# Read-out tokens' first product as seven products, and the P runs of batches 0 and 1 regrouped

## The chip, the cores and the metric

The kernel runs on one core of a Trainium2 chip. The metric is the device time in microseconds of one execution; the median over several executions is given. The engines are TensorE (PE, matmuls; PEld, its weight loads), VectorE (DVE), ScalarE (ACT), GpSimd (POOL) and SyncE (SP, which here only issues DMAs). A matmul takes both operands from SBUF and writes to PSUM, which has eight banks of 128 x 512 float32; ACT and DVE read results out of PSUM.

## The reference

A cross-attention block between tokens `x` (8 batches, 8 heads, 512 tokens, 64 wide) and states `state` (8, 8, 32, 64), followed by a two-layer network with exact GELU over all 8 x (512 + 32) = 4352 rows of width 512:

```python
a = softmax(scale * x @ state.T);   xread = a @ state     # 512 rows per batch
a2 = softmax(scale * state @ x.T);  sread = a2 @ x        # 32 rows per batch
x2 = concat([xread, sread], axis=2)  # heads side by side: width 512
out = gelu(x2 @ w_in) @ w_out        # w_in 512 x 2048, w_out 2048 x 512
```

The 32 `sread` rows of each batch are called the read-out tokens: 256 over the whole problem.

## The kernel before, in words

**Tokens of x.** For a batch b the kernel never forms `xread`. It forms `P = state @ w_in` (`p_mm`, lines 415 to 428: 64-row, 32-column pieces of the array, one chunk `f` is 512 of the 2048 columns, two PSUM tiles per chunk) and copies it to SBUF in bf16 (`p_copy`: one half on ACT, one on DVE). `mm1` (line 460) multiplies a block of 128 columns of P with the transposed attention weights AT and applies GELU on ACT, giving `g`. `M(k, k+1)` is two such blocks. For batch 0 the second layer is the plain `mm2` or `mm2_m` (lines 486 and 515); `U(n)` is four matmuls of it. From batch 1 on the second layer is done with **seven products instead of eight** (Strassen's way, after Winograd: halves of the tokens, of the inner dimension and of the columns give 2 x 2 x 2 blocks; sums of blocks are multiplied). `X(b, name)` (line 599) is one of the seven, 16 matmuls of 128 x 256; `g_sum` (line 565) makes its left sum on DVE for every batch, `w_sums` (line 542) made the right sums once. Its evacuations add and subtract the products.

**Read-out tokens.** `sread` (line 378) computes them per batch, `sread_out` normalises, and `srt` (line 405) transposes them into `XSR`, which holds all 256 tokens as [128, 4 chunks of the model width, 32, 8]. After batch 7's are there, `mm1_sr(m)` (line 503) multiplies `w_in` with `XSR`: for each of 16 blocks of 128 columns, four matmuls of 128 x 256, then a GELU of 256 columns into `g_sr`. `R(name)` (line 734) does the second layer of the read-out tokens, again as seven products, from sums made by `r_sum`.

**Order.** Tiles are placed by pools that hand out buffers in a ring; the order of instructions on each engine is the order in which the program writes them, and each engine works through its own queue in order. PSUM has two families: `ftile` hands out four banks in turn (tag "f": `hp` of `mm1`, `p_ps`, `sr`, transposes, `st_ps`, `hps`), and `otile` the other four (accumulators of `mm2`, X and R). An instruction on PE that takes a bank waits until the last reader of what was there is done. Lines 809 to 943 write the order for batches 0 and 1 by hand; the loop of lines 945 to 1024 does batches 2 to 7 in eight slots p = 0 to 7 each, a slot being `M(k, k+1)` and one X product of the batch before. In batch 7 the slots p = 0 to 3 hold four calls of `mm1_sr` each, and p = 5 to 7 the R products.

**Early part that the change touches.** `p_run(1, (0, 1), ...)` makes chunks 0 and 1 of batch 1 (16 small matmuls, four "f" banks), `pmat(0, 3)` chunk 3 of batch 0, `pmat(1, 2)` chunk 2 of batch 1, with `mm2_m`, `atr(1)` (transposes of batch 1's attention weights), `M` and `srt(1)` between. `state_prep(2, 3)` transposes states into the "f" tile `st_ps` and copies them to `sbd` on DVE (line 165). `w_sums(0)` is a DVE sum that needs all of `w_out` (line 540), whose last quarter comes by the last DMA that `load_rest` issues. A block of P must be copied before the `mm1` that reads it: chunk 3 of batch 0 before M(12), chunk 0 of batch 1 before M(16), chunk 1 before M(20).

Of the kernel before, what the change touches and what calls it, by code (L numbers as in the profile page):

```python
# [9 lines left out]
FP32 = mybir.dt.float32  # L10
# [7 lines left out]
def kernel(  # L18
# [8 lines left out]
    nc = tc.nc  # L27
# [33 lines left out]
    def ftile(shape, name):  # L61
        return ps_f.tile(shape, FP32, name=name, tag="f")
# [297 lines left out]
    def atr(b, ts=(0, 1)):  # L360
        A = atts[b]
        if 0 in ts:
            A.AT = att.tile([128, SJ, 2, 128], BF16, name="AT", tag="AT")
        for t in ts:
            ps = ps_f.tile([128, SJ, 128], BF16, name="aT_ps", tag="f")
            for j in range(SJ):
                nc.tensor.transpose(ps[:, j, :], A.a[:, 2 * j + t, :], ident)
            nc.vector.tensor_copy(out=A.AT[:, :, t, :], in_=ps)
# [36 lines left out]
    def srt(b):  # L405
        A = atts[b]
        ps = ps_f.tile([128, HC, NS], BF16, name="srT", tag="f")
        nc.tensor.transpose(
            ps.rearrange("p c n -> p (c n)"), A.srm.rearrange("q t d -> q (t d)"), ident
        )  # L410
        nc.vector.tensor_copy(out=XSR[:, :, :, b], in_=ps)
# [23 lines left out]
    def pmat(b, f):  # L435
        p_copy(b, f, p_mm(b, f, ftile))

    def pmat00(h):
        if h == 0:
            Ps[0] = att.tile([128, 2, d_ff], BF16, name="P", tag="P")
        ps = [otile([128, 256], "p_ps") for t in range(2)]
        for c in range(HC):
            for t in range(2):
                nc.tensor.matmul(
                    ps[t][32 * c:32 * c + 32, :],
                    lhsT=sbd[64 * t:64 * t + 64, 0, c, 32 * t:32 * t + 32],
                    rhs=w_in_bf[64 * t:64 * t + 64, c, 256 * h:256 * h + 256],  # L450
                    start=True,
                    stop=True,
                )
        for t in range(2):
            nc.scalar.copy(out=Ps[0][:, t, 256 * h:256 * h + 256], in_=ps[t])
# [30 lines left out]
    def mm2(b, q, j):  # L486
# [11 lines left out]
        if q == 3:  # L498
            rows = out_rows(b, j)
            h = d_model // 2 if j == SJ - 1 else d_model  # L500
            evac(ps, [(rows[:, n:n + h], slice(0, 128), n, n + h) for n in range(0, d_model, h)])

    def mm1_sr(m):
        hp = ps_f.tile([128, B * NS], FP32, name="hps", tag="f")
        for c in range(HC):
            nc.tensor.matmul(  # L506
                hp,
                lhsT=w_in_bf[:, c, m * 128:(m + 1) * 128],
                rhs=XSR[:, c, :, :].rearrange("p n b -> p (n b)"),
                start=(c == 0),  # L510
                stop=(c == HC - 1),
            )
        nc.scalar.activation(out=g_sr[:, m, :], in_=hp, func=AF.Gelu)

    def mm2_m(b, m):
        for j in range(SJ):
            if m == 0:
                ops[b, j] = otile([128, d_model], "op")
            nc.tensor.matmul(  # L519
                ops[b, j],  # L520
                lhsT=gs[b][:, m, j * 128:(j + 1) * 128],
                rhs=w_out_bf[:, m, :],
                start=(m == 0),
                stop=(m == MC - 1),
            )
# [64 lines left out]
    def c22(b):  # L590
        xs[b, "v"] = c_tile("v")
        o = xs[b, "o", 1]
        nc.gpsimd.tensor_tensor(  # L593
            out=xs[b, "v"], in0=xs[b, "q"], in1=o[:, :, :NH], op=ALU.subtract
        )
        nc.vector.tensor_tensor(out=o[:, :, NH:], in0=xs[b, 3], in1=xs[b, "v"], op=ALU.add)  # L596
        x_out(b, 1)

# [103 lines left out]
    def L7():  # L702
        b = B - 1
        for j, n0, n1, at in PIECES:
# [4 lines left out]
            )  # L709
            rows_out(0, slice(j, j + 1), slice(n0, n1), nc.scalar if n0 else nc.sync)  # L710

    rs = {}

    def r_q(h, k):
# [86 lines left out]
    def M(*ms):  # L801
        for m in ms:
            mm1(m // MC, m % MC)

    def U(*us):
        for u in us:
            mm2(u // 16, u % 16 // 4, u % 4)

    begin(0)
    begin_e(0)  # L810
    keep_warm(31)
# [80 lines left out]
    sread_out(1)  # L892
    M(10, 11)
    mm2_m(0, 8)
    p_run(1, (0, 1), (None, None))
    mm2_m(0, 9)
    atr(1)
    pmat(0, 3)
    mm2_m(0, 10)
    M(16, 17)  # L900
    srt(1)
    M(12, 13)
    mm2_m(0, 11)
    begin(2)
    rearr(2)
# [4 lines left out]
    w_sums(0)  # L910
    M(14, 15)
    state_prep(2, 3)
    pmat(1, 2)
    U(12)
    begin(3)
    rearr(3)
# [28 lines left out]
    for b in range(2, B):  # L945
        nb = b + 1
        for p in range(8):
            k = 16 * b + 2 * p
            if p == 1 and nb < B:
                scores(nb, 0)  # L950
                scores(nb, 1)
            if p in (2, 3) and nb < B:
                norm(nb, p - 2)
            if p == 3 and nb + 1 < B:
                xtr_dma(nb + 1)
            if p == 5 and nb < B:
                atr_dma(nb)
            if p == 7 and nb < B:
                srt(b)
                if nb == B - 1:  # L960
                    srt(nb)
            M(k, k + 1)
            if b == 2 and p in (0, 3):
                pmat(2, 2 + p // 3)
            if b == 2 and p == 1:
                w_sums(4)
            if p < 5:
                if p == 0:
                    g_sum(b - 1, "5")
                X(b - 1, "45127"[p])  # L970
                if p < 3:
                    g_sum(b - 1, "127"[p])
            if nb == B and p < 4:
                for m in range(4 * p, 4 * p + 4):
                    mm1_sr(m)
            if p == 0 and b + 3 < B:
                hold_for(b, 0)
                load_x(4 if b == 2 else b + 3)
            if p == 6 and b == 2:
                hold_for(b, 12)  # L980
                load_x(5)
            if p == 0 and nb + 1 < B:
                begin(nb + 1)
                rearr(nb + 1)
            if nb == B:
                if p == 4:
                    r_homes()
                    r_sum("5")
                    r_sum("2")
                if p == 5:  # L990
                    g_sum(b, "6")
                    R("3")
                    r_sum("1")
                    R("4")
                    r_sum("6")
                    r_sum("7")
                if p == 6:
                    R("5")
                    X(b, "3")
                    R("2")  # L1000
                    R("1")
# [64 lines left out]
```

The softmax here doesn't subtract the row's maximum and nothing guards it: scores larger than these inputs give would overflow.

## Time and profile before

| | |
|---|---|
| median of 3 executions | 206.5 us (205.84 to 212.98) |
| the profiled execution | 206.31 us, of which 204.5 us from the first to the last instruction (the span) |
| PE, DVE, ACT, POOL busy | 97%, 70%, 66%, 34% of the span |
| `mm1_sr`'s 64 matmuls | first at 162.8, last at 177.5 us |
| granted TensorE clock | 1.00 throughout |

The page of a profile lists the busy time of each engine, then the span in 40 slices (a digit is the busy share in tenths), the DMA queues, the chain of work that ended last, the costliest groups of instructions and the DMA issues. A group's line gives the source line, the engine and operation, output and inputs by name, shapes, the number of instructions, their busy time and mean length, and what ended the idle time before them. Matmuls are pipelined: a matmul's own length contains its way through the array, so cost is read from the distance between starts, or from the chain, which counts each stretch once.

### The profile page before, as it was taken

What the parts mean: (1) busy time and instruction counts of PE and PEld (TensorE: products, weight loads), DVE (VectorE), ACT (ScalarE), POOL (GpSimd) and SP (SyncE); (2) the same over time, 40 slices, a digit from 0 to 9 for tenths busy, and PEclk for the clock granted to TensorE, in tenths of its full rate; (3) what the DMA queues carried; (4) which work ended last, traced back from release to release, by engine and by line L of the source; (5) the groups of instructions that cost most, each with busy time, mean ns of one, the idle gap of its engine ahead of it and who ended that gap; (6) DMA issues with size and microseconds to landing.
All of it is one profiled execution on the core that took longest, in us unless ns stands there. A gap on an engine that the chain in (4) does not pass through costs nothing.

```text
span 204.5 us, 4754 instructions
## 1 busy us (share of the span) xinstructions
PE 197.9 (97%) x1984; PEld 133.3 (65%) x1989; DVE 142.9 (70%) x227; ACT 134.0 (66%) x242; POOL 69.6 (34%) x76
## 2 busy tenths in 40 slices
PE   7799999999999999999999999999999999999993
PEld 2344444446777577766776687567775887778893
DVE  2953896689898959976797757765778543175882
ACT  3784685799686779666967596678857376744120
POOL 8983305334239546370527502420220011200000
PEclk9999999999999999999999999999999999999999
DMA  6999996995585788755783309470117001030125
GB/s 191 206 176 204 206 199 102 154 219 105 116 144 103 208 103 106 155 169 39 83 169 140 76 0 113 147 109 0 51 39 169 3 0 51 3 154 0 54 103 155
DMA packets 40565, 23.14 MB, mean 113 GB/s; under 512 B 21856, under 2 KB 39136, under 8 KB 40544
## 3 DMA queue, kind: packets, MB, share of 16 engines
q0 software_dynamic: 13984, 8.10, 29.7%
q1 hardware_dynamic: 25872, 14.36, 28.9%
q10 hardware_dynamic: 688, 0.39, 0.6%
q8 instruction: 15, 0.25, 0.5%
q14 instruction: 6, 0.05, 0.1%
HBM read 17.30 MB, written 8.91 MB: 128 GB/s over the span
## 4 chain that ended last, share of the span: by engine, by line
PE 88%; DMA 6%; DVE 2%; ACT 1%; POOL 0%; issue 0%; SPq 0%; DVEq 0%
PE xp L574 41%; PE hp L465 25%; PE p_ps L421 5%; DMA xb<-in_x_dram 4%; PE hps L506 3%; PE rp L750 3%; PE op L519 3%; DMA x0f<-in_x_dram 2%; PE op L491 2%; PE xp L680 2%; PE pt L330 2%; PE sr L384 1%; DVE a L353 1%; DVE cs L350 1%; PE xT_ps L256 1%; PE xT_ps L270 1%
## 5 line engine op out<-in xcount | busy, mean ns | idle before, releaser
L472 ACT ACTIVATE g<-hp 128x512 bf16<-128x512 f32 x124 | 67.3, 604 | 28.4 <-PE hp L465 21.6
L465 PE MATMUL hp<-AT,P 128*128 128x512 bf16 x248 | 63.6, 379 | 0.0
L574 PEld LDWEIGHTS <-gsum 128*128 128x128 bf16 x528 | 51.2, 98 | 13.1 <-issue 1.9
L568 DVE TENSOR_TENSOR gsum<-g 128x2048 bf16<-128x2048 bf16 x35 | 45.9, 1328 | 0.1
L574 PE MATMUL xp<-ws,gsum 128*128 128x256 bf16 x304 | 36.3, 273 | 0.0
L465 PEld LDWEIGHTS <-P 128*128 128x128 bf16 x248 | 22.9, 98 | 19.9 <-issue 2.8
L574 PE MATMUL xp<-ws,g 128*128 128x256 bf16 x224 | 26.8, 273 | 0.0
L574 PE MATMUL xp<-w_out_bf,gsum 128*128 128x256 bf16 x224 | 26.6, 273 | 0.0
L574 PEld LDWEIGHTS <-g 128*128 128x128 bf16 x224 | 21.8, 98 | 5.1 <-issue 0.2
L433 DVE CAST P<-p_ps 128x512 bf16<-128x512 f32 x30 | 19.6, 685 | 7.3 <-PE p_ps L421 7.2
L623 POOL TENSOR_TENSOR u<-s,oh 128x512 f32<-128x512 f32 x6 | 8.9, 1490 | 40.7 <-ACT oh L620 40.7
L224 POOL COPY x<-xb 128x1024 bf16<-128x1024 bf16 x12 | 13.1, 1118 | 21.0 <-DMA xb<-in_x_dram 21.0
L432 ACT CAST P<-p_ps 128x512 bf16<-128x512 f32 x30 | 16.8, 601 | 4.7 <-PE p_ps L421 4.3
L234 POOL COPY xo<-xb 128x1024 bf16<-128x1024 bf16 x12 | 14.7, 1251 | 4.4 <-PE sr L384 4.4
L593 POOL TENSOR_TENSOR v<-q,oh 128x512 f32<-128x512 f32 x6 | 8.8, 1460 | 20.8 <-ACT oh L625 17.6
L617 DVE TENSOR_TENSOR s<-xp,s 128x512 f32<-128x512 f32 x6 | 4.1, 691 | 11.3 <-PE xp L574 11.3
L519 PE MATMUL op<-w_out_bf,g 128*128 128x512 bf16 x45 | 11.4, 380 | 0.2
L421 PE MATMUL p_ps<-w_in_bf,sbd 64*32 64x512 bf16 x248 | 11.4, 383 | 0.1
L353 DVE TENSOR_TENSOR a<-e,ics 128x512 bf16<-128x512 bf16 x14 | 10.9, 782 | 0.5
L596 DVE TENSOR_TENSOR oh<-xp,v 128x512 f32<-128x512 f32 x6 | 4.1, 691 | 9.8 <-POOL v L593 9.8
L629 DVE TENSOR_TENSOR q<-xp,s 128x512 f32<-128x512 f32 x6 | 4.1, 684 | 8.0 <-PE xp L574 8.0
L350 DVE TENSOR_REDUCE cs<-e 128x16 f32<-128x512 bf16 x14 | 9.5, 676 | 0.0
(111 smaller groups left out, 217.4 us busy)
## 6 DMA issues: line engine op xcount, KB each, us to landing
out_dram<-oh SPq DMA_DIRECT2D x15, 256.0 KB, 2.4
xb<-in_x_dram POOLq DMA_DIRECT2D x7, 512.0 KB, 6.1
out_dram<-oh SPq DMA_DIRECT2D x6, 512.0 KB, 3.1
w_in_bf<-in_moe_w_in_dram POOLq DMA_DIRECT2D x6, 256.0 KB, 10.5
out_dram<-osb SPq DMA_DIRECT2D x5, 256.0 KB, 4.7
w_out_bf<-in_moe_w_out_dram POOLq DMA_DIRECT2D x4, 256.0 KB, 7.7
w_out_bf<-in_moe_w_out_dram POOLq DMA_DIRECT2D x2, 512.0 KB, 12.5
x0f<-in_x_dram SPq DMA_DIRECT2D x3, 256.0 KB, 3.9
```

Of the source, the lines that this page charges most:

```text
L224: nc.gpsimd.tensor_copy(out=A.x4[:, :, :, 64 * t:64 * t + 64].rearrange("p j c d -> p c j d"), in_=src[:, t],)
L234: eng.tensor_copy(out=A.xo[:, :, :, 2 + 64 * t:66 + 64 * t].rearrange("p j c d -> p c j d"), in_=src[:, t],)
L350: nc.vector.reduce_sum(out=cs, in_=e4, axis=AX.X)
L353: nc.vector.tensor_tensor(out=A.a[:, :, hs].rearrange("p g (c n) -> p g c n", n=NS), in0=e4, in1=ics[:, :, :].to_broadcast((128, G, 2, NS) ...
L421: nc.tensor.matmul(ps[t][32 * c:32 * c + 32, :], lhsT=sbd[64 * t:64 * t + 64, b, c, 32 * t:32 * t + 32], rhs=w_in_bf[64 * t:64 * t + 64, c ...
L432: nc.scalar.copy(out=dst[:, 0, :], in_=ps[0])
L433: nc.vector.tensor_copy(out=dst[:, 1, :], in_=ps[1])
L465: nc.tensor.matmul(hp, lhsT=Ps[b][:, t, m * 128:(m + 1) * 128], rhs=atts[b].AT[:, :, t, :], start=(t == 0), stop=(t == 1),)
L472: nc.scalar.activation(out=gs[b][:, m, :], in_=hp, func=AF.Gelu)
L519: nc.tensor.matmul(ops[b, j], lhsT=gs[b][:, m, j * 128:(j + 1) * 128], rhs=w_out_bf[:, m, :], start=(m == 0), stop=(m == MC - 1),)
L568: nc.vector.tensor_tensor(out=t, in0=g_q(b, h0, k0), in1=g_q(b, h1, k1), op=op)
L574: nc.tensor.matmul(ps[:, j - js[0], :], lhsT=lhs[:, m, 128 * j:128 * j + 128], rhs=rhs[:, m, :], start=(first and j == js[0] and m == 0), ...
```

## The change

The first product of the read-out tokens, 2048 x 512 times 512 x 256, is done by seven products of halves as well: halves of `d_ff` (h), of the model width (k) and of the tokens (n). `SR(name, g)` is one product of one group g of 512 of a half's 1024 columns: four blocks by two chunks of the model width, so eight matmuls of 128 x 128 into one "f" bank. ACT copies products 3, 5 and 2 out of PSUM, DVE forms the sums, and `SR_gelu` applies GELU to 512 columns at once from SBUF. `sr_w` makes the sums of `w_in` blocks (two DVE operations per name; four names in the slots p = 0 of batches 3 to 6, "7" in batch 7), `sr_x` the sums of tokens. `read_out_slot` writes the order of p = 0 to 4 in batch 7. There the DVE addition of `c22` comes later than before (`c22_add`). It is for fewer multiplications: 112 matmuls of 128 columns in place of 64 of 256.

In batches 0 and 1 `burst` makes chunks (0, 3) and (1, 0) together, after one more `mm2_m`, and (1, 1) and (1, 2) together: two runs of 16 small matmuls in place of one of 16 and two of 8. M(12, 13) then comes ahead of M(16, 17).

```diff
+    def burst(chunks, b_read=None):
...
+        for i, (b, f) in enumerate(chunks):
+            done.append((b, f, p_mm(b, f, ftile if i < 2 else otile)))
+        for x in done[:2]:
+            p_copy(*x)
...
+    def sr_w(name):
...
+        (h0, k0), (h1, k1), op = G_SUMS[name]
+        for g in range(2):
+            nc.vector.tensor_tensor(
+                out=homes[g], in0=sr_wq(h0, k0, g), in1=sr_wq(h1, k1, g), op=op
+            )
...
+    def SR(name, g):
+        bank = {"3": 0, "4": 1, "5": 0, "2": 1, "1": 2, "6": 3, "7": 2}[name]
+        first = name in "3416"
+        if first:
+            sr[bank] = ftile([128, 4, TH], "sp")
...
+        for i in range(4):
+            for k in range(2):
+                nc.tensor.matmul(
+                    ps[:, i, :],
+                    lhsT=lhs[:, k, 128 * i:128 * i + 128],
+                    rhs=rhs[:, k, :],
+                    start=(first and i == 0 and k == 0),
+                    stop=(k == 1),
+                    skip_group_check=True,
+                )
+        tt, add, sub = nc.vector.tensor_tensor, ALU.add, ALU.subtract
+        a, u = sr["a"], sr["u"]
+        if name == "3":
+            nc.scalar.copy(out=a, in_=ps)
+        elif name == "5":
+            nc.scalar.copy(out=sr["uc"], in_=ps)
+            tt(out=u, in0=a, in1=sr["uc"], op=sub)
+        elif name == "2":
+            nc.scalar.copy(out=sr["ac"], in_=ps)
+            tt(out=a, in0=a, in1=sr["ac"], op=sub)
+        elif name == "7":
+            tt(out=u, in0=ps, in1=u, op=add)
+        else:
+            tt(out=a, in0=ps, in1=a, op=add)
...
+        if p == 0:
+            sr_x("34")
+            M(k, k + 1)
+            g_sum(c, "5")
+            sr_w("7")
+            SR("3", 0)
+            SR("4", 0)
+            sr_x("167")
+            X(c, "4")
+            SR("5", 0)
+            SR("2", 0)
+            g_sum(c, "1")
+        if p == 1:
+            M(k, k + 1)
+            SR_gelu("52", 0)
+            X(c, "5")
+            SR("1", 0)
+            SR("6", 0)
+        if p == 2:
+            M(k, k + 1)
+            SR_gelu("6", 0)
+            SR("7", 0)
+            SR_gelu("7", 0)
+            g_sum(c, "2")
+            X(c, "1")
+            SR("3", 1)
+            SR("4", 1)
+            g_sum(c, "7")
+        if p == 3:
+            M(k, k + 1)
+            SR("5", 1)
+            SR("2", 1)
+            SR_gelu("52", 1)
+            X(c, "2")
+            SR("1", 1)
+            SR("6", 1)
+        if p == 4:
+            M(k, k + 1)
+            SR_gelu("6", 1)
+            SR("7", 1)
+            SR_gelu("7", 1)
+            c22_add(c)
+            X(c, "7")
...
     mm2_m(0, 8)
-    p_run(1, (0, 1), (None, None))
     mm2_m(0, 9)
+    burst([(0, 3), (1, 0)])
+    mm2_m(0, 10)
     atr(1)
-    pmat(0, 3)
-    mm2_m(0, 10)
+    M(12, 13)
+    srt(1)
     M(16, 17)
-    srt(1)
-    M(12, 13)
     mm2_m(0, 11)
...
     M(14, 15)
     state_prep(2, 3)
-    pmat(1, 2)
+    burst([(1, 1), (1, 2)])
     U(12)
...
                     g_sum(b - 1, "5")
+                    if b > 2:
+                        sr_w("5216"[b - 3])
                 X(b - 1, "45127"[p])
...
-            if nb == B and p < 4:
-                for m in range(4 * p, 4 * p + 4):
-                    mm1_sr(m)
```

More of the change, by code (lines that the diff above doesn't have):

```diff
@@ L436, in pmat @@
         p_copy(b, f, p_mm(b, f, ftile))
+    def burst(chunks, b_read=None):
+        done = []
+        first = len(chunks) < 4 and b_read is not None
+        if first:
+            sread(b_read)
+        for i, (b, f) in enumerate(chunks):
+            done.append((b, f, p_mm(b, f, ftile if i < 2 else otile)))
+        for x in done[:2]:
+            p_copy(*x)
+        if b_read is not None and not first:
+            sread(b_read)
+        for x in done[2:3]:
+            p_copy(*x)
+        if b_read is not None:
+            sread_out(b_read)
+        for x in done[3:]:
+            p_copy(*x)
     def pmat00(h):
@@ L501, in mm2 @@
             evac(ps, [(rows[:, n:n + h], slice(0, 128), n, n + h) for n in range(0, d_model, h)])
[L503 to L513, printed above, removed]
     def mm2_m(b, m):
@@ L595, in c22, with c22_add @@
         )
+        if b < B - 2:
+            c22_add(b)
+    def c22_add(b):
+        o = xs[b, "o", 1]
         nc.vector.tensor_tensor(out=o[:, :, NH:], in0=xs[b, 3], in1=xs[b, "v"], op=ALU.add)
@@ L710, in L7, with sr_wq, sr_xq @@
             rows_out(0, slice(j, j + 1), slice(n0, n1), nc.scalar if n0 else nc.sync)
+    sr = {}
+    FH = d_ff // 2
+    TH = B * NS // 2
+    SR_W = {"3": (0, 0), "4": (1, 1)}
+    def sr_wq(h, k, g):
+        return w_in_bf[:, 2 * k:2 * k + 2, FH * h + 512 * g:FH * h + 512 * g + 512]
+    def sr_xq(k, n):
+        return XSR[:, 2 * k:2 * k + 2, 16 * n:16 * n + 16, :].rearrange("p c n b -> p c (n b)")
+    def sr_w(name):
+        if name in "52":
+            homes = [opool.tile([128, 2, 512], BF16, name="srw", tag="osb") for _ in range(2)]
+        elif name == "7":
+            t = att.tile([128, 2, 2, 512], BF16, name="srw7", tag="xT")
+            homes = [t[:, 0], t[:, 1]]
+        else:
+            t = x4s["16".index(name)].rearrange("p j c n -> p (j c n)")
+            t = t.rearrange("p (g k f) -> p g k f", g=2, k=2)
+            homes = [t[:, 0], t[:, 1]]
+        (h0, k0), (h1, k1), op = G_SUMS[name]
[3 more added lines that the diff above has]
+            )
+            sr["w" + name, g] = homes[g]
@@ new lines, in sr_x @@
+    def sr_x(names):
+        for name in names:
+            if "x" not in sr:
+                t = att.tile([128, 4, 2, TH], BF16, name="srx", tag="e")
+                one = att.tile([128, 2, TH], BF16, name="srx1", tag="a")
+                sr["x"] = dict(zip("34167", [t[:, i] for i in range(4)] + [one]))
+            (k0, n0), (k1, n1), op = {
+                "3": ((0, 1), (1, 1), ALU.subtract),
+                "4": ((1, 0), (0, 0), ALU.subtract),
+                "6": ((0, 0), (0, 1), ALU.add),
+                "1": ((0, 0), (1, 1), ALU.add),
+                "7": ((1, 0), (1, 1), ALU.add),
+            }[name]
+            nc.vector.tensor_tensor(
+                out=sr["x"][name], in0=sr_xq(k0, n0), in1=sr_xq(k1, n1), op=op
+            )
@@ new lines, in sr_g @@
+    def sr_g(h, n, g):
+        return g_sr[:, MH * h + 4 * g:MH * h + 4 * g + 4, TH * n:TH * n + TH]
+    def SR(name, g):
+        bank = {"3": 0, "4": 1, "5": 0, "2": 1, "1": 2, "6": 3, "7": 2}[name]
+        first = name in "3416"
+        if first:
+            sr[bank] = ftile([128, 4, TH], "sp")
+        if name == "3":
+            for i in "au":
+                t = xin.tile([128, 2, 4, TH], FP32, name="srt", tag="xb")
+                sr[i], sr[i + "c"] = t[:, 0], t[:, 1]
+        ps = sr[bank]
+        lhs = sr_wq(*SR_W[name], g) if name in SR_W else sr["w" + name, g]
+        rhs = {"5": sr_xq(1, 1), "2": sr_xq(0, 0)}.get(name)
+        rhs = sr["x"][name] if rhs is None else rhs
+        for i in range(4):
[7 more added lines that the diff above has]
+                    skip_group_check=True,
+                )
+        tt, add, sub = nc.vector.tensor_tensor, ALU.add, ALU.subtract
+        a, u = sr["a"], sr["u"]
+        if name == "3":
+            nc.scalar.copy(out=a, in_=ps)
[5 more added lines that the diff above has]
+            tt(out=a, in0=a, in1=sr["ac"], op=sub)
+        elif name == "7":
+            tt(out=u, in0=ps, in1=u, op=add)
+        else:
+            tt(out=a, in0=ps, in1=a, op=add)
@@ L712, with SR_gelu @@
+    def SR_gelu(names, g):
+        for name in names:
+            home, h, n = {"5": ("uc", 0, 1), "2": ("ac", 1, 0), "6": ("a", 1, 1), "7": ("u", 0, 0)}[name]
+            nc.scalar.activation(out=sr_g(h, n, g), in_=sr[home], func=AF.Gelu)
     rs = {}
@@ L807, in U, with read_out_slot @@
             mm2(u // 16, u % 16 // 4, u % 4)
+    def read_out_slot(p):
+        c, b, k = B - 2, B - 1, 16 * (B - 1) + 2 * p
+        if p == 0:
[41 more added lines that the diff above has]
+            X(c, "7")
     begin(0)
@@ L961 @@
                     srt(nb)
+            if nb == B and p < 5:
+                read_out_slot(p)
+                if p == 4:
+                    r_homes()
+                    r_sum("5")
+                    r_sum("2")
+                continue
             M(k, k + 1)
@@ L985 @@
             if nb == B:
[L986 to L989, printed above, removed]
                 if p == 5:
```

## The prediction

> **What bounds the kernel now.** I read the busy shares and the clock first.
>
> ```profile
> PE 197.9 (97%) x1984; PEld 133.3 (65%) x1989; DVE 142.9 (70%) x227; ACT 134.0 (66%) x242; POOL 69.6 (34%) x76
> PEclk9999999999999999999999999999999999999999
> ```
>
> TensorE (PE) is busy 97% at full clock. Busy time of pipelined matmuls overstates, so next came the chain that ended last, in order of time (start, length, what).
>
> ```profile
> 29.09 0.30 DVE srm L398
> 29.43 0.41 PE p_ps L421 x8
> 29.84 0.97 PE op L519 x4
> 30.81 0.45 PE aT_ps L367 x8
> 31.26 0.34 PE p_ps L421 x8
> 31.60 0.97 PE op L519 x4
> ...
> 36.08 0.06 PE st_ps L159
> 36.13 0.60 PE p_ps L421 x8
> 36.74 0.97 PE op L491 x4
> ...
> 153.38 0.56 PE p_ps L421 x16
> ...
> 162.99 1.75 PE hps L506 x16
> ...
> 197.85 3.55 PE xp L680 x48
> ```
>
> From about 30 us to the end nearly every link is PE, so what counts is PE time added or removed, and any new wait of PE. Four prices are in these lines. A 128x256 matmul takes 1.75/16 = 109 ns. L680 is 16 of those plus 32 of 128x128: (3.55 - 1.75)/32 = 56 ns each. A P run of 8 takes 0.34, one of 16 takes 0.56. The matmuls beside a run pay for it: four of 128x512 take 0.86 elsewhere and 0.97 next to one, so 0.11 a run.
>
> The timeline of the two stretches (start, length, and idle before with its releaser) shows who makes PE wait early on, and how free VectorE (DVE) is later:
>
> ```profile
> 29.43 0.11 PEld L421 LDWEIGHTS <-sbd 64*32 64x32 bf16 x8 [0.43 <-DVE srm L398]
> 34.45 1.23 DVE L540 TENSOR_TENSOR ws<-w_out_bf 128x2048 bf16<-128x2048 bf16 x1 [0.20 <-DMA w_out_bf<-in_moe_w_out_dram]
> 36.17 0.46 DVE L165 COPY sbd<-st_ps 64x128 bf16<-64x128 bf16 x2 [0.49 <-PE st_ps L159]
> 163.02 0.69 DVE L617 TENSOR_TENSOR s<-xp,s 128x512 f32<-128x512 f32 x1 [2.53 <-PE xp L574]
> ```
>
> **What the skill says.** "TensorE: Matmul & The Clock Gate", section Back-to-back issue gap, gives about 81 ns as the sustained spacing of N=128 matmuls that each load weights. The trace disagrees: each of the 32 above loads its own weights, at 56 ns. "TensorEngine Tiling (Array Packing)", Key Properties: changing the tiling mode drains the engine; the 0.11 beside a run agrees. "VectorE: DVE Perf Modes", Side-by-side: a two-source bf16 op makes two elements a cycle. L568 (2048 elements, 1.22 us) and L726 (1024, 0.69) agree. "SBUF — State Buffer", Who interferes with whom: an op with two SBUF inputs and a GpSimd op that reads SBUF shut each other out. By the line view of L568 from 70 to 84 us one of them beside GpSimd's copies lasts 2.93 us instead of 1.21.
>
> **Part 1, the read-out product.** Removed: 64 matmuls of 128x256, four times 1.75 = 6.99 us, all on the path. Added: 7 products x 2 groups x 8 matmuls = 112 of 128x128 at 56 ns = 6.26. They use the full array like their neighbours, so no switch. Net on PE: **-0.73 us**, if PE never waits.
>
> DVE gets ten weight sums of 1024 elements (L726's form, 0.69, two in 1.29), five token sums of 256 (about 0.3 each, estimated from L398's 0.29 for 128 elements and L764's 0.42 for 256 in f32), and 12 evacuations of 512 f32 (0.69). Eight weight sums go into the first slot of batches 3 to 6, after g_sum 5. There DVE idles until the next product: 3.41 between starts of g_sum and L617, less 1.2, leaves 2.2 us, and 1.29 fits. The tightest is batch 3, where the lengthened L568 ends 0.2 before its product; the sums run before that op and before GpSimd's copy, so I cost them at nothing.
>
> The last two sums, the token sums and the evacuations, about 11 us of DVE, fall between 160 and 180 us, where DVE is busy 3.45 and 2.51 of 10 us by windows: some 17 of 20 after. ScalarE (ACT) swaps 16 GELUs of 256 (four in 1.64) for 8 of 512 and 6 copies (0.6 each, 0.49 apart): 6.6 becomes about 7.
>
> Does a wait arise? I walked the slots from the start of p=0, with 0.22 from a product's end to its reader's start. SR 3 ends at 1.31, SR 4 at 1.76. ACT is in its two GELUs until about 1.7, so the copy of 3 ends near 2.3, 4's evacuation near 3.0. X 4 fills PE until 3.50 and SR 5 until 3.95, so SR 2, which adds onto 4's bank, finds it free with 0.9 to spare. SR 1 and 6 start at 7.0 and 7.5; their banks came free at 4.8 and 5.3. In p=2 and p=3 it is tighter: 4's second evacuation queues behind g_sum 2 and q, ends near 12.95, and SR 2 starts at 13.16. The last GELU of g_sr ends near 19.1 and R 3 reads it at 20.2. No wait, but 0.2 in one place: 0 to 0.3 as bounds, 0 taken. c22's addition moves behind SR 7 so that DVE does not stand waiting for GpSimd; nothing on PE reads it.
>
> **Part 2, the P runs.** Before: a run of 16, one of 8, one of 8. After: two of 16. The first burst comes one unit of mm2_m (0.86) later. srm, which held a bank of the run at 28.89 (timeline) until 29.4, is then done before 29.76, so that wait of 0.33 goes. The run of 8 at 31.26 goes with its switches: 0.34 + 0.11 = 0.45. Burst 1 needs w_in's last quarter; its last issue is at 16.1 and the longest landing 12.9, so 29.05: in time by 0.7. P(0,3) is copied by about 31.0 and M(12) wants it at 31.6; A's transposed copies end at 32.4 and M(16) now comes at 32.55. So up to state_prep PE gains 0.78: st_ps at 35.14 instead of 35.91.
>
> Then burst 2 needs all four "f" banks: those of M17, M14, M15 and st_ps. The last comes free after DVE's two copies (0.46), which queue behind w_sums(0), and that op waited for the **landing of w_out's last quarter at 34.43**, which PE does not move. It still runs 34.45 to 35.68, the copies end near 36.1, the second half of the burst starts near 36.12 and ends 0.34 later, at 36.46. Before, this point was 36.67. Gain **0.2** here, not 0.8: about 0.6 goes into a wait. Bounds: 0.1 (copies and their signal 0.1 later) and 0.82 (no wait: 0.33 + 0.45 + the old wait of 0.26 - 0.22 for the longer run). From U(12) on each operation follows the same ones as before, so the shift stays.
>
> **Sum.** 0.73 + 0.2 = 0.93 us off the span. The median of before is 206.5, so 205.6.
>
> **Rivals.** (a) *Both gains without a wait*: 0.73 + 0.82 = 1.55, so 204.9. For it: my landing comes from one trace, and an earlier landing by 0.5 gives this. Against: L540 names the DMA. (b) *The evacuations hold PE up*: 12 DVE ops in series with ACT copies, with 0.2 to spare in one place. If each of four products waits 0.2, Part 1 gives nothing and Part 2 gives 0.2: 206.3. Against: DVE and ACT were half idle, and each product's partner is X, which needs nothing of them. (c) *Weights bound the small matmuls*: at the skill's 81 ns, 112 take 9.07, which is 2.1 more than the 6.99 removed; 206.5 + 2.1 - 0.2 = 208.4, slower than before. For it: bursts of 8 with other neighbours than L680. Against: L680 itself.
>
> **How the numbers follow.** Forecast 0.62, (a) 0.12, (b) 0.20, (c) 0.06. Predicted 205.6. The range holds the forecast with its bounds, (a) and (b), and some 0.4 for the scatter of one median (205.84 and 206.5 are two runs of one kernel): 204.6 to 206.9. 2% is 4.1 us; no case comes near it: same 0.98, faster 0.01, slower 0.01.
>
> **What would show it.** SR groups of 16 matmuls in about 0.9 us, no idle of PE before them: Part 1 right; gaps released by DVE or ACT mean (b), 81 ns spacing means (c). A wait inside the second burst until L165's copies end: Part 2 right; without it, (a). X groups still 1.75 long and back to back. I am wrong if DVE's new work delays a g_sum of batches 3 to 6, which would show as PE idle before an X product.

## The result and the profile after

| | before | after |
|---|---|---|
| median, same chip | 206.17 us (4 executions, 205.69 to 212.98) | 212.26 us (4 executions, 211.46 to 213.93) |
| ratio | | 1.029, 95% interval 1.021 to 1.038 |
| span of the profiled execution | 204.5 us | 210.6 us |

One of the four executions before took 212.98 us, the other three 205.69 to 206.50. The forecast was 205.6 us, in a range from 204.6 to 206.9. The changed kernel is 3% slower, so the forecast was wrong by 6.7 us, and in its direction.

The page of the kernel after, busy shares and granted clock, shows it at a glance: PE is busy for longer, but for 95% of the span instead of 97%, and in the ninth and tenth slices (a slice is 5.3 us, so from 42 to 53 us) the clock is not full.

```profile
PE 199.8 (95%) x2032; PEld 134.2 (64%) x2037; DVE 157.1 (75%) x254; ACT 135.9 (65%) x240; POOL 69.0 (33%) x76
PEclk9999999967999999999999999999999999999999
```

The chain of the kernel after that ended last, in order of time, names what stands there (start, length, what):

```profile
34.22 0.09 POOL hold L901
34.30 10.17 DMA xT<-x
44.48 0.05 issue
44.52 1.03 PE pt L330 x16
45.56 1.71 PE op L510 x4
47.26 0.56 PE p_ps L421 x5
...
167.96 0.89 PE sp L787 x16
168.85 1.75 PE xp L581 x16
170.60 0.89 PE sp L787 x16
171.49 0.86 PE hp L484 x4
...
203.84 3.55 PE xp L692 x48
```

For 10.17 us this chain, on which the end of the kernel hangs, is a DMA: `xtr_dma(2)`, by which SyncE transposes the tokens of batch 2 from SBUF to SBUF (`xT<-x`). `scores(2, 0)`, the transposes and products at L330, reads it. The four matmuls after it take 1.71 us where they take 0.86 elsewhere: half speed. Further down, 16 matmuls of the new product take 0.89 us, as forecast.

In the source, `xtr_dma(2)` is followed by `hold_for(0, 13)`, `load_x(3)` and `load_st(3, B)`. The hold is a one-column copy on GpSimd that reads what GELU 13 of batch 0 (that of block 13) wrote. It keeps the two loads behind it in GpSimd's queue until then: the tokens of batch 3, 512 KB, and some states, 160 KB. The diff does not touch these four lines. But it moves M(12, 13) ahead of M(16, 17), and GELU 13 with it. First the timeline of the kernel before, GpSimd and SyncE (start, length; for a DMA the length is that of its issue):

```profile
35.16 0.57 POOL L798 COPY hold<-g 128x1 bf16<-128x1 bf16 x1 [1.17 <-ACT g L472]
35.68 0.88 POOL L117 DMA_DIRECT2D xb<-in_x_dram  x1
...
34.02 2.06 SPq L277 DMA_TRANSPOSE xT<-x  x1
```

And the timeline of the kernel after, with the lines of DVE and PE that the second burst of P and the scores depend on:

```profile
34.22 0.19 POOL L901 COPY hold<-g 128x1 bf16<-128x1 bf16 x1
34.34 0.88 POOL L117 DMA_DIRECT2D xb<-in_x_dram  x1
...
34.30 3.43 SPq L277 DMA_TRANSPOSE xT<-x  x1
...
34.78 1.23 DVE L547 TENSOR_TENSOR ws<-w_out_bf 128x2048 bf16<-128x2048 bf16 x1 [1.18 <-DMA w_out_bf<-in_moe_w_out_dram]
...
36.43 0.41 PE L421 MATMUL p_ps<-w_in_bf,sbd 64*32 64x512 bf16 x8 [0.35 <-DVE sbd L165]
...
44.52 1.03 PE L330 MATMUL pt<-sbd,xT 128*128 128x64 bf16 x16 [4.13 <-DMA xT<-x]
```

Before, the hold waited 1.17 us for its GELU and the load was issued 1.66 us after the transposing DMA. Now the hold finds the GELU done and waits for nothing, and load and transposing DMA are issued 0.04 us apart. The transposing DMA landed 4.4 us after its issue before, and 10.2 us after it now; these are the lines of the DMA view, before and then after, with the median time from issue to landing at the end:

```profile
xT<-x SPq DMA_TRANSPOSE x1, 4.4
```

```profile
xT<-x SPq DMA_TRANSPOSE x1, 10.2
```

PE waits 4.13 us for it.

The windows of the kernel after show the second half of the damage (stretch, length, busy time of PE, PEld, DVE, ACT, POOL, then granted clock, DMA share, GB/s; a DMA share above 1 means that packets of one DMA engine overlap in the record):

```profile
42.00:44.00 2.00, 0.00 (x0) 0.00 (x0) 0.00 (x0) 0.00 (x0) 0.00 (x0) 0.80 1.60 257
...
48.00:50.00 2.00, 2.00 (x6) 0.75 (x5) 1.97 (x4) 1.89 (x3) 0.00 (x0) 0.50 0.34 131
50.00:52.00 2.00, 1.84 (x16) 0.73 (x16) 1.90 (x5) 1.84 (x4) 0.00 (x0) 1.00 0.00 0
```

The clock halves at 43.2 us, during the wait, and is back at 50.0 (both by windows of 0.2 us).

Taken together, by starts of the same instructions in the two traces (stretches that differ by nothing are in part left out):

| stretch | before, us | after, us | difference |
|---|---|---|---|
| first instruction to M(10, 11) | 27.02 | 27.13 | +0.10 |
| M(10, 11) to U(12): both bursts of P | 9.646 | 9.642 | 0.00 |
| M(20, 21) to scores of batch 2: wait for `xT` | 0.86 | 5.15 | +4.29 |
| scores of batch 2 to X 3 of batch 1: half clock | 5.04 | 7.37 | +2.33 |
| X 3 of batch 1 to M of p = 0 in batch 7: batches 2 to 6 | 115.04 | 115.04 | 0.00 |
| M of p = 0 to M of p = 5 in batch 7: read-out product | 20.037 | 19.304 | -0.73 |
| the end | | | +0.1 |
| sum | | | +6.1 |

The sum is the difference of the spans (210.6 - 204.5) and of the medians (212.26 - 206.17 = 6.09).

In batch 7 the windows from 168 to 174 us of the kernel before and, after it, of the kernel after tell of the new work (same columns; the changed kernel is 6.7 us later here, so the two do not show the same slots):

```profile
168.00:174.00 6.00, 6.00 (x50) 4.72 (x49) 1.82 (x2) 4.10 (x12) 1.27 (x1) 1.00 0.12 44
```

```profile
168.00:174.00 6.00, 6.00 (x70) 5.17 (x68) 4.96 (x10) 4.05 (x9) 0.00 (x0) 1.00 0.00 0
```

DVE's busy time rises from 1.82 to 4.96 us of 6 while PE stays full.

### The profile page after: what moved, and what is told of

Same layout as the page of the kernel before. It is cut to its first block, busy times and chain, and to the rows that moved or that the text cites. A ratio compares the mean times of both kernels' runs of the same rounds, so it can differ in the third digit from the quotient of the medians.

```text
span 210.6 us, 4898 instructions
## 1 busy us (share of the span) xinstructions
PE 199.8 (95%) x2032; PEld 134.2 (64%) x2037; DVE 157.1 (75%) x254; ACT 135.9 (65%) x240; POOL 69.0 (33%) x76
## 4 chain that ended last, share of the span: by engine, by line
PE 80%; DMA 15%; POOL 2%; DVE 1%; issue 1%; ACT 0%
PE xp L581 39%; PE hp L484 23%; DMA xb<-in_x_dram 5%; DMA xT<-x 5%; DMA w_out_bf<-in_moe_w_out_dram 4%; PE p_ps L421 4%; PE sp L787 3%; PE rp L853 3%; PE xp L692 2%; PE warm_ps L149 2%; PE pt L330 2%; PE op L510 1%; PE sr L384 1%; POOL x L224 1%; DVE xT L260 1%
## 5 line engine op out<-in xcount | busy, mean ns | idle before, releaser
L484 PE MATMUL hp<-AT,P 128*128 128x512 bf16 x248 | 64.5, 385 | 0.0
L581 PE MATMUL xp<-ws,g 128*128 128x256 bf16 x224 | 26.8, 273 | 0.0
L224 POOL COPY x<-xb 128x1024 bf16<-128x1024 bf16 x12 | 12.6, 1080 | 22.3 <-DMA xb<-in_x_dram 22.3
L624 ACT COPY s<-xp 128x512 f32<-128x512 f32 x7 | 4.1, 586 | 7.7 <-PE srT L408 4.4
```

Source lines behind the costliest of these rows:

```text
L224: nc.gpsimd.tensor_copy(out=A.x4[:, :, :, 64 * t:64 * t + 64].rearrange("p j c d -> p c j d"), in_=src[:, t],)
L484: nc.tensor.matmul(hp, lhsT=Ps[b][:, t, m * 128:(m + 1) * 128], rhs=atts[b].AT[:, :, t, :], start=(t == 0), stop=(t == 1),)
L581: nc.tensor.matmul(ps[:, j - js[0], :], lhsT=lhs[:, m, 128 * j:128 * j + 128], rhs=rhs[:, m, :], start=(first and j == js[0] and m == 0), ...
```

## The experiments

My theory after the result: the load of batch 3's tokens, issued together with the transposing DMA, makes that DMA land about 6 us later; PE's wait and the half clock that it brings on are the whole of the loss; the read-out product and the bursts of P are not slower themselves. The rivals: the new order of the early batches delays the scores in another way; the transposing DMA is slow by its own later or slower issue (SyncE took 3.43 us for it instead of 2.06); the read-out product costs time that the comparison of two traces hides.

Below, "lag" is the time from the issue of the transposing DMA to that of the load of `x`, and "M(10) to X 3" the time from the start of M(10, 11) to that of X 3 of batch 1, which holds everything that happens early: 18.15 us before, 24.77 after. Ratios are to the kernel before, with 95% intervals.

### The load later, in the changed kernel

```diff
     xtr_dma(2)
-    hold_for(0, 13)
-    load_x(3)
-    load_st(3, B)
     w_sums(0)
     M(14, 15)
+    hold_for(0, 15)
+    load_x(3)
+    load_st(3, B)
     state_prep(2, 3)
```

> The changed kernel with one move: the load of batch 3's x (and of the states) is held until the GELU of block 15 instead of block 13, so it is issued about 1.9 us after the transposing DMA of batch 2 instead of together with it. Theory T (the early load and the transposing DMA share the DMA engines, scores of batch 2 wait for it, and the idle PE then loses its clock): the wait of 4.1 us and the slow clock go, xT lands about 4.4 us after its issue as before the change, and the time is 205.2 to 205.7. Rival R1 (the transposing DMA is late for another reason that comes with the new order, such as the later landing of w_out or a changed SyncE queue): the wait stays, 211 to 213.

Measured: 205.73 us, ratio 0.996 (0.994 to 0.998). Lag 2.2 us, `xT` landed 4.4 us after its issue, PE does not wait for it, the clock is full. Three lines, moved and set to GELU 15, take away 6.5 us. The rest of the change stands as it was, so neither the order nor the read-out product is what made it slower.

### The load earlier, in the kernel before

```diff
     xtr_dma(2)
-    hold_for(0, 13)
+    hold_for(0, 11)
     load_x(3)
```

> The kernel before with one move the other way: the load of batch 3's x waits for the GELU of block 11 instead of 13, so GpSimd issues it right after its two copies, at about 34.1 us, together with the transposing DMA. PE's order, the P runs and the read-out product stay as before. Theory T: xT lands some 10 us after its issue, PE waits about 4 us and then runs at half clock, 211 to 213. Rival R1: nothing happens, 206.

Measured: 211.9 us, ratio 1.028 (1.024 to 1.032). One number in the old kernel makes it 5.5 us slower. The waits of PE from 34 us on (total, times, longest), and the timeline, in this run:

```profile
PE pt L330 <- DMA xT<-x: 4.6, 1, 4.6
```

```profile
33.79 3.19 SPq L277 DMA_TRANSPOSE xT<-x  x1
...
33.82 0.88 POOL L117 DMA_DIRECT2D xb<-in_x_dram  x1
```

Lag 0.03 us, landing 10.6 us after the issue. The clock is at half from 45.3 to 48.7 us. Here too SyncE takes 3.19 us for the issue: the long issue comes with the collision and does not need the new order.

### The read-out product alone

The changed kernel with the early order of the kernel before:

```diff
     mm2_m(0, 8)
+    p_run(1, (0, 1), (None, None))
     mm2_m(0, 9)
-    burst([(0, 3), (1, 0)])
-    mm2_m(0, 10)
     atr(1)
-    M(12, 13)
-    srt(1)
+    pmat(0, 3)
+    mm2_m(0, 10)
     M(16, 17)
+    srt(1)
+    M(12, 13)
...
-    burst([(1, 1), (1, 2)])
+    pmat(1, 2)
     U(12)
```

> The read-out product by seven products alone: batches 0 and 1 in the old order. By the prediction's Part 1 and theory T: 0.73 us less than before, 205.4; the transposing DMA lands as before. Rival R2 (the read-out part, or its DVE sums in batches 3 to 6, costs something that the profile hides): 206.2 or more.

Measured: 205.72 us, ratio 0.997 (0.994 to 1.000); M(10) to X 3 took 18.147 us, as before. Part 1 is worth 0.3%, which is what 0.73 of 206 us makes (0.35%), though the interval reaches almost to no difference.

> The read-out product by seven products alone, again: 0.7 us below the kernel before (the saving of PE counted from the trace is 0.73).

Measured in a second comparison: 207.25 us, ratio 0.999 (0.995 to 1.002). This one is inconclusive: in the profiled execution the last quarter of batch 0's tokens landed at 8.16 us instead of about 6.4, the clock was at half from 10.95 to 14.37 us, and everything after began 1.7 us later. The edit touches nothing there. Both intervals hold 0.35%, and the second holds no difference as well, so the times alone don't show Part 1's gain; the traces do.

### PE kept busy during the wait

```diff
     M(20, 21)
+    ps = otile([128, 512], "warm_ps", 3)
+    for i in range(20):
+        nc.tensor.matmul(ps, lhsT=warm[:, 0:128], rhs=warm, start=True, stop=True)
     scores(2, 0)
```

The changed kernel, with 20 products of zeros that nothing reads.

> The changed kernel with 20 matmuls of 128x512 on zeros put before the scores of batch 2 (4.3 us of PE work that nothing needs), so that PE is busy while it waits for the transposing DMA. It sizes the part of the loss that is the clock's. Theory T with the clock as a second cause: the wait is now work and stays in the time, but the matmuls after it run at full clock, so 2.3 us less than the changed kernel: 209.5 to 210.2. If the clock plays no part: 212 or more.

Measured: 210.01 us, ratio 1.017 (1.014 to 1.020). PE's timeline in this run:

```profile
39.86 4.48 PE L1071 MATMUL warm_ps<-warm 128*128 128x512 bf16 x20
44.41 0.64 PE L330 MATMUL pt<-sbd,xT 128*128 128x64 bf16 x16
44.88 1.03 PE L510 MATMUL op<-w_out_bf,g 128*128 128x512 bf16 x4
```

`xT` lands as late as in the changed kernel, and PE still starts the scores at 44.4 us, but the 16 transposes take 0.64 instead of 1.03 us, and scores to X 3 takes 4.82 instead of 7.37. So 2.5 us of the loss were the clock: 6.09 - (210.01 - 206.41) = 2.49; by starts it is 7.37 - 4.82 = 2.55. The remaining 3.60 is the wait, 4.55 by starts (44.41 - 39.86), less the read-out product's 0.73 and the 0.22 by which 4.82 is below the 5.04 of before.

### The states early, the tokens late

```diff
     hold_for(0, 13)
-    load_x(3)
     load_st(3, B)
     w_sums(0)
     M(14, 15)
+    hold_for(0, 15)
+    load_x(3)
     state_prep(2, 3)
```

> The changed kernel with the two loads taken apart: the small load of the states (160 KB) stays early, that of batch 3's x (512 KB) is held until the GELU of block 15. If the volume of the x load is what slows the transposing DMA: 205.5 to 206, xT lands some 4.4 us after its issue. If any load from GpSimd's queue that starts together with it does: xT lands at about 44 again, 211 or more. In between (an xT some 1 to 2 us later, still in time for its scores at 40): no loss of time, but seen in the landing.

Measured: 206.8 us, ratio 1.002 (0.999 to 1.004). The 160 KB load of states, 0.03 us behind the transposing DMA, is enough to spread its data until 40.11 us, 2 us more than with the load later. By then the packets of the tokens, issued 2.45 us behind it, have begun as well (39.86 us), and `xT` lands 7.9 us after its issue, so the end of this delay is not the states' alone. It is more than the expectation had in between, and PE does wait. The waits of PE and the window from 42 to 44 us in this run:

```profile
PE pt L330 <- DMA xT<-x: 1.9, 1, 1.9
```

```profile
42.00:44.00 2.00, 1.82 (x29) 0.94 (x30) 0.28 (x1) 1.26 (x1) 0.00 (x0) 1.00 1.23 272
```

After a wait of 1.9 us the clock is still full. Here the short wait costs only itself; the long one of the changed kernel costs half as much again.

### How much lag is needed

In the changed kernel, two idle copies (or one) of 512 columns on GpSimd between hold and load put the load off without touching anything else:

```diff
     hold_for(0, 13)
+    for _ in range(2):
+        nc.gpsimd.tensor_copy(out=warm, in_=xbs[2].rearrange("p h f -> p (h f)")[:, 0:512])
     load_x(3)
```

> The changed kernel with two idle copies of 512 columns on GpSimd between the hold and the load of batch 3's x, which do nothing but let about 1.1 us pass; PE's order is that of the changed kernel. The load is then issued some 1.1 to 1.3 us after the transposing DMA (0.04 in the changed kernel, 2.2 with the later load). If overlap is what counts: the transposing DMA has moved over half of its data before the load's packets come, lands about 6 to 7.5 us after its issue (between 4.4 and 10.2), PE waits 0.5 to 1.5 us, and the time is 206 to 207.3. If it is all or nothing: 4.4 or 10.2 us again, 205.6 or 212.

Measured with two: the copies took 2.16 us, twice what I had meant. Timeline:

```profile
33.70 2.16 POOL L1057 COPY warm<-xb 128x512 bf16<-128x512 bf16 x2
35.81 0.88 POOL L117 DMA_DIRECT2D xb<-in_x_dram  x1
```

Lag 2.14 us, landing after 4.36 us, no wait, 206.2 us, ratio 0.996 (0.993 to 0.999). Nothing is moved on PE, ACT or DVE here; putting off the load alone removes the loss.

> As the run with two idle copies, with one: there the load came 2.14 us after the transposing DMA and did not touch it (4.36 us to landing), so a lag between 0.04 and 1.66 us is still open. One copy should give about 1.1 us. If the two slow each other only where their data overlap: the load's first data come some 1.7 us after its issue, so about 2.8 us after the transposing DMA's issue, when about two thirds of the latter's are through: landing after 5 to 7 us, 0 to 1 us of waiting on PE, 205.8 to 207. If even then nothing is slowed: 4.4 us and 205.8 to 206.2. If the order of issue decides: 10 us and 212.

Measured with one copy (`range(1)`): it took 0.61 us, lag 0.59, landing after 9.1 us, PE waits 3.0 us, 209.45 us, ratio 1.015 (0.996 to 1.034, of two executions only, so the time is loose; the trace is not). The DMA view of this run, by queue (packets, MB, share of 16 engines), is the most telling of all. `q1` is SyncE's queue with the transposing DMA, `q0` GpSimd's with the load. From 35.2 to 38.5 us, and then from 38.6 to 42.0:

```profile
q1 hardware_dynamic: 2048, 0.52, 86.7%
q0 software_dynamic: 85, 0.04, 16.1%
...
q0 software_dynamic: 1014, 0.44, 123.0%
q1 hardware_dynamic: 25, 0.00, 1.0%
```

By 38.5 us all 2048 packets (512 KB) of the transposing DMA are through, 3.0 us after the first of them, against 2.7 in the kernel before. What is missing is 32 packets of 4 bytes, which would be two for each of the 16 DMA engines. I take them for the completion signals: in the kernel before they run from 37.70 to 38.02 us, and `xT` counts as landed at 38.47. Here the first runs at 39.53 us, 25 of them get through by 42.0 among 1014 packets of GpSimd's loads, and `xT` lands at 43.18. If the small packets are the signals, the data was there, and the word that it was there came 4.8 us later. The expectation, 5 to 7 us and at most 1 us of waiting, had only the overlap of data in it.

So the lag between issues is only a proxy. The record of single packets, run by run:

| run | lag, us | data packets of `xT`, us | mean packet, ns | first packet of the load, us | landing, after the last data packet | landing, after the issue |
|---|---|---|---|---|---|---|
| load later | 2.2 | 35.41 to 38.03 | 22.0 | 38.13 | 0.5 | 4.4 |
| two copies | 2.14 | 34.94 to 37.54 | 22.0 | 37.67 | 0.5 | 4.4 |
| before | 1.66 | 35.29 to 37.97 | 21.9 | 37.90 | 0.5 | 4.4 |
| one copy | 0.59 | 35.36 to 38.38 | 22.3 | 38.07 | 4.8 | 9.1 |
| states early | 0.03 (states; tokens 2.45) | 35.53 to 40.11 | 26.8 | 37.25 | 2.0 | 7.9 |
| after | 0.04 | 35.64 to 42.46 | 36.2 | 36.77 | 2.0 | 10.2 |
| before, load earlier | 0.03 | 35.13 to 42.17 | 35.0 | 36.07 | 2.3 | 10.6 |

In these runs a load whose packets come once data and signals are through does no harm. One that comes in the middle stretches the packets from 22 to 35 or 36 ns, spreads the data over 7 us instead of 2.7, and the signals come late; with one that comes just at the end the signals alone are late. Packets can be slow for another reason, too: in the second run of the read-out product alone they took 28 ns, and `xT` landed after 4.9 us, though no packet of the load was there yet. The kernel before was at the edge: its load's first packet came at 37.90 us, when 26 of the 32 signals had gone.

### The second burst without its wait

The load later, as in the first experiment, and the second burst put behind M(18, 19) and U(12), so that what it waits for is done (the lines that go in front of `w_sums(0)` are left out here):

```diff
     M(14, 15)
+    hold_for(0, 15)
+    load_x(3)
+    load_st(3, B)
     state_prep(2, 3)
-    burst([(1, 1), (1, 2)])
+    M(18, 19)
     U(12)
+    burst([(1, 1), (1, 2)])
...
     w_sums(1)
-    M(18, 19)
     U(13)
```

> The kernel with the later load, and the second burst moved behind M(18, 19) and U(12), so that it no longer stands at the bank of the state transposes, which waits for w_sums(0) and with it for w_out's last quarter. In the run with the later load alone this burst took 1.48 us instead of 0.56. If that wait is what ate Part 2's gain, some 0.8 us come back (0.1 is given to the copies of P that M(20) needs): 204.8 to 205.2. Rival R3 (batches 0 and 1 are held by something else, such as the landing of xT at 38.4 or the exponentials on ScalarE): 205.7, as with the later load alone.

Measured: 205.28 us, ratio 0.993 (0.989 to 0.996); M(10) to X 3 took 17.34 us, 0.81 less than before.

> The later load with the second burst behind M(18, 19) and U(12), again: if the wait of that burst ate Part 2's gain, 0.4 to 0.8 below the later load alone; if not, equal to it.

Measured again: 205.03 us, ratio 0.991 (0.989 to 0.994); 17.33 us. Expected from the traces is (0.73 + 0.82) / 206.4 = 0.75%. Both intervals hold it. This kernel is faster than the kernel before by both intervals, and than the changed one.

> The later load again, beside the two that follow on one chip, to tell fractions of a us apart. If Part 2 with its wait behind w_out's last quarter is worth nothing: equal to the read-out part alone within 0.15 us. If it is worth the 0.2 that was forecast or more: 0.2 or more below it.

The load later, measured again beside it: 205.82 us, ratio 0.994 (0.992 to 0.997); M(10) to X 3 18.005 us. Its interval overlaps that of the read-out product alone in the same comparison (0.995 to 1.002), so the times don't decide what Part 2 was worth. The burst moved as well is 0.79 us below it, as expected. The chains in order of time, first of the load later, then of the burst moved as well, show the difference:

```profile
35.05 1.23 DVE ws L547
36.28 0.12 DVE sbd L165
36.40 0.01 issue
36.42 0.24 DVE sbd L165
36.66 0.04 issue
36.70 0.41 PE p_ps L421 x8
```

```profile
36.25 0.22 PE op L510
...
36.52 0.59 PE op L510 x2
37.11 0.56 PE p_ps L421 x16
37.67 0.97 PE op L510 x4
```

In the first, the second half of the burst stands behind `w_sums(0)` (L547) and the copies of `sbd`; in the second the 16 matmuls run through in 0.56 us and DVE is off the chain.

> As the run with the later load, but held until the GELU of block 14: the load is then issued about 0.5 us sooner, some 1.6 us after the transposing DMA instead of 2.2 (0.04 in the changed kernel, 1.66 in the kernel before). If the collision is a matter of overlap, xT lands between 38.4 and 39.5 and the time is 205.5 to 206; if the order of issue alone matters, 4.4 us to landing as in the run with the later load.

A hold on GELU 14 instead of 15 was to give a lag of some 1.6 us. It gave 205.96 us, ratio 0.996 (0.993 to 1.000), but in the profiled execution the last quarter of batch 0's tokens again landed late (8.14 us), PE ran 1.7 us late, and the lag came out as 3.1 us, so it says nothing of the threshold. `xT` landed after 4.5 us.

All runs with the burst in the changed place also say what sets its length. `w_out`'s last quarter lands some tenths before `state_prep` starts, and the sum on DVE runs from the landing:

| run | landing ahead of `state_prep`, us | second burst, us |
|---|---|---|
| load later | 0.38 | 1.48 |
| after | 0.49 | 1.37 |
| PE kept busy | 0.53 | 1.33 |
| states early | 0.54 | 1.32 |
| one copy | 0.61 | 1.31 |
| load later, again | 0.64 | 1.23 |
| two copies | 0.81 | 1.12 |
| hold on GELU 14 | 1.71 | 1.09 |

Each tenth of landing is about a tenth of burst, down to 1.1 us, where something else takes over (I think the bank that GELU 15 reads, which ends some 0.85 us after `state_prep` starts; not tried).

## Why the prediction was wrong, point by point

**The step that failed** is a half sentence at the end of Part 2: "From U(12) on each operation follows the same ones as before, so the shift stays." On PE that is so. Off PE, the hold in front of `load_x(3)` names GELU 13, and Part 2 moves GELU 13 ahead of M(16, 17). I followed what each PE instruction waits for, and what it frees for PE and DVE, but not who else reads its result. The reader was a one-column copy whose only purpose is to time a DMA. No rival held it either: all three were about PE, DVE and weights. The three experiments on the load (later in the new kernel, earlier in the old one, two idle copies) show this cause from both sides. It makes +4.29 us of wait and +2.33 of half clock.

The half clock could have been priced. The Trainium skill, "TensorE: Matmul & The Clock Gate", section What's actually happening, says that the clock halves after an idle window of about 3.4 us, that the window runs freely, and that a busy window brings it back. The runs agree in the main: half clock for 6.8 us in the changed kernel (43.2 to 50.0) and 3.4 us with one copy (43.1 to 46.5), two windows and one, and none after an idle of 1.9 us. In the kernel before with the load earlier it lasted 3.4 us as well, and began at 45.3, 0.8 us after PE had resumed: start and length go by the window, not by the wait. The traces show the grid of the windows: the clock falls once more after the last work of PE, in the changed kernel at 210.44 us, in the old one with the load earlier at 209.10, and from the first fall (43.19, 45.26) that is 49.0 and 48.0 times 3.413 us. Three windows of this grid in the changed kernel (stretch, length, busy time of PE, clock, DMA share, GB/s):

```profile
39.78:43.19 3.41, 0.61 (x3) 1.00 1.61 184
43.19:46.60 3.41, 2.08 (x19) 0.50 0.72 160
46.60:50.01 3.41, 3.41 (x16) 0.50 0.20 77
```

A wholly idle window was not needed: the clock fell after a window with 0.61 us of busy PE, after 0.78 with the load earlier and 0.50 with one copy. Over the traces of all runs it fell after windows with up to 2.0 us and held in some with 1.4, so busy time alone doesn't decide it. It came back only after windows with 2.8 us or more, and not after the one with 2.08 shown here. So the 2.33 us are partly chance: they depend on where the windows happened to lie.

**Part 1 was right.** Forecast -0.73 on PE, measured -0.73 between M of p = 0 and M of p = 5. 16 matmuls take 0.89 us, 56 ns each, and no wait of PE stands before them, so neither the rival of evacuations nor that of weights at 81 ns came about. DVE was forecast busy 17 of 20 us; from M of p = 0 to M of p = 5 it was busy 16.1 of 19.3, by windows. The weight sums in batches 3 to 6 cost nothing: batches 2 to 6 took 115.04 us in both.

**Part 2 had the right mechanism and a wrong size.** The first burst gave what was forecast up to `state_prep`, within a tenth: forecast 35.14, seen 35.25, of which 0.10 is the later start. The second burst does wait for the copies of `sbd` behind `w_sums(0)`, which the chain and the 0.35 us before the second eight show. The term that was mis-sized is the **landing of `w_out`'s last quarter**: I took 34.43 from one trace as fixed, and it was 34.76 in the changed kernel. That 0.33, of which 0.10 is the later start of everything, turned the gain of 0.2 into 0.00. Over all runs the landing is uncertain by more than the gain was, and by M(10) to X 3 Part 2 was worth from -0.42 us (the load later, 18.57 against 18.15) over +0.15 (the same again) and +0.26 (two copies) to +0.28 (hold on GELU 14). In the first of these the first burst waited as well, for another landing (timeline of the weight loads):

```profile
29.52 0.14 PEld L421 LDWEIGHTS <-sbd 64*32 64x32 bf16 x15 [0.23 <-DMA w_in_bf<-in_moe_w_in_dram]
```

I had put the last quarter of `w_in` at 29.05 and "in time by 0.7", again from one trace. It landed at 29.48 in that run, at 29.77 with the states early, where the burst waited too, and at 29.45 in the changed kernel, 0.4 ahead of need. My lower bound of 0.1 had no allowance for either landing. The upper bound, 0.82 without a wait, is what the moved burst reached: 0.81 and 0.82.

**The rivals.** Rival (a), 204.9 us, is about what the kernel gives with load and burst moved (205.03 and 205.28 us). The versions with the changed order whose load comes 2 us or more behind the transposing DMA all have medians in the range of 204.6 to 206.9 us.

**What stays open.** Why the load's packets pass ahead of the others was not tried. The Trainium skill, "DMA: Bandwidth & Descriptors", section Queues, rings and completion order, says that each DMA engine takes turns between queues and drains a whole packet, typically 9 to 17 descriptors, before it switches. If the entries of the record are descriptors, a turn of 17 at 64 ns (with one copy, 301 entries of the load took 119.8% of 16 engines from 39 to 40 us) is 1.1 us by estimate (0.9 if one entry in 53 ns is taken, which is what 301 in 1 us on 16 engines come to), and the first signal came 1.15 us after the last data packet. But the last of the 32 came 4.5 us after it (42.86), some four such turns for two packets an engine. So the first fits and the last doesn't, and all of it is an argument. Whether the signals wait for a turn or for data of the load that was under way was not tried. Nor was a lag between 0.59 and 1.66 us tried, and whether GELU 15 sets the floor of the second burst.

## What to carry to other kernels

When a change moves an instruction, list every reader of its result on every engine, one-element copies that only time a DMA first of all, and ask what the DMA they release will then run beside. A transfer that is on the path (here one whose reader has 1.7 us to spare) wants the queue to itself until its completion is signalled, not only until its data is through. If PE must wait, the wait's length can matter twice: by M(20, 21) to X 3 of batch 1, a wait of 1.9 us cost 1.8, one of 3.0 cost 4.4 and one of 4.1 cost 6.6.

## What the runs showed of the hardware that I had not expected

- A 512 KB transposing DMA from SBUF to SBUF takes 4.4 us from issue to landing (4.9 in one run) when the load comes 1.66 us or more behind it, and 10.2 to 10.6 with 672 KB of loads (tokens and states) started beside it. With 160 KB beside it, and the rest 2.45 us behind, it is 7.9.
- Its data packets can be through 4.8 us before it counts as landed: 32 packets of 4 bytes come late, among the packets of the other queue.
- SyncE's issue of it takes 3.2 to 3.4 us with both loads started beside it, 2.5 with the states alone, and otherwise 2.0 to 2.4; it is 2.0 with the load 0.59 us later, though `xT` lands late there as well.
- A half clock lasted 3.4 or 6.8 us. It fell and rose on a grid of 3.413 us, and it began once 2.8 us into an idle of PE and once 0.8 us after one.
- Two GpSimd copies of 128 x 512 took 2.16 us together, and one alone, in another run, 0.61.
